# Moving VectorE's side work behind a step's products, and one modulation into the second cycle

## The chip, the cores and the metric

One core of one Trainium2 chip runs the program. The metric is the device time of one execution in microseconds (us). A kernel is timed by the median of its executions; for the kernel before there are three, with a median of 704.68 us (703.97 to 706.22).

## The reference: what is computed

A block with adaptive layer normalization: a state-space convolution over 2048 tokens of 448 channels, then a token-mixing MLP. Six vectors that scale and shift (`sa, ca, ga, sb, cb, gb`, here `mod[0]` to `mod[5]`) come from one condition vector.

```python
mod = (_silu(c) @ w_mod).reshape(c.shape[0], 6, 1, -1)
sa, ca, ga, sb, cb, gb = (mod[:, 0], ..., mod[:, 5])
h = _layernorm(x, axis=-1) * (1 + ca) + sa
x = x + ga * _A_ref(h, ...)     # y = irfft(rfft(u) * rfft(K)), K = 2 Re sum_n C_n exp(A_n dt t)
h = _layernorm(x, axis=-1) * (1 + cb) + sb
x = x + gb * _B_ref(h, ...)     # (W2 gelu(W1 LayerNorm(h)^T))^T over tokens
```

## The kernel before, in words

The convolution's kernel K has 256 complex exponentials for each of 448 channels and 2048 positions. The program makes it in 56 steps `s`, in seven cycles of eight; a step makes the tables of 16 channels for one half of their exponentials. Spectra are multiplied later. A cycle opens with a window (`window(s)`, s a multiple of 8), in which ScalarE (ACT) makes eight magnitudes `mag` by Exp, so that its function table is changed once; then follow eight steps that use Sin. In step s

- `st_abs(s)` and the first lines of `st_step(s)` (L640, L641, L650 to L653) run on ACT: from the phases `xe` and `xg` in PSUM they make two tables `gs` in SBUF and, in place, sines and cosines in `xe` and `xg`;
- GpSimd (POOL) multiplies `mag` by the two `gs` into `G` (L655, L656), and makes the next-but-one step's squared table `m` (`st_mag2`, L630, L632; also called m2);
- VectorE (DVE) makes the four products E(s): two from the sine `xe` (L657, L658), two from the cosine `xg` (L662, L663);
- TensorE (PE) makes kg from E and G of step s-2 (`st_kgen`, L686, 32 small matmuls) and then the phases of step s+1 (`st_phase`, L603). Phase tiles have two PSUM buffers each, so phase s+1 writes where phase s-1 stood, and has to wait for the last product E(s-1) that reads it.

PE, ACT, DVE and POOL issue in the order in which the program is written (a manual schedule). An instruction that waits therefore holds all that stands behind it on its engine. SyncE's DMA queue (SP) is written by hand up to step 8, and ordered by the scheduler after that.

Beside the products there is other work. `between()` in `main`'s loop flushes pending DVE pieces (`dve`: the skip term `ks` L705, rows `yt` L532), takes the statistics of rows of x (`u_stats`, two instructions L503 and L504 a row; 16 rows, the first four in window 0), and advances by `more(n)` a chain of some 50 small DVE instructions that prepares the next parameters (L393 to L452). In the first cycle `between()` stands between the second and the third product of a step; in the second cycle and from step 32 on it stands behind the fourth (`behind`). The statistics of all rows end in `rs` on ACT (L464, L465) and `nm` on DVE (L508 to L512) at the head of window 8; from there POOL and ACT normalize the rows (`u_norm`, L519, L517), PE transforms them (`u_rows`, L529, `pu`) and DVE multiplies them into `yt`.

`modulation(k, *halves)` makes `mod[k]`: two matmuls a half on PE (L490) against a 784 KB slice `wm` of `w_mod`, into one PSUM tile, and one ACT instruction behind the second half (L494). That tile is one of three buffers (`pms`) that `pu` and the second transform `y1` (L724) share. The slices are loaded by `wm_load` (L326), from POOL's queue in the first cycle, into four slots or, late, into rows of the tile `xt` that held x. A row of x is loaded with others by `x_load` (L301), on POOL's queue too.

Of the kernel before, what the change touches and what calls it, by code (L numbers as in the profile page):

```python
# [30 lines left out]
BATCH = 8  # L31
# [194 lines left out]
def tile_adaln_s4d_mixer(ctx, tc, i, out):  # L226
    nc = tc.nc
# [19 lines left out]
    with ExitStack() as es:  # L247
        V, S, G, T = nc.vector, nc.scalar, nc.gpsimd, nc.tensor
# [40 lines left out]
        PP = 112  # L289
# [6 lines left out]
        xt = xp.tile([P, 16, D], F32, name="xt")  # L296
# [27 lines left out]
        def wm_load(k, tile, eng=nc.sync):  # L324
            wms[k] = tile
            eng.dma_start(wms[k], i["w_mod"][:, k * D : (k + 1) * D].rearrange("(q p) d -> p q d", p=PP))  # L326

        s2_v = i["S2"].rearrange("p (k m) -> p k m", k=32)
        svt = sp2.tile([P, 17], F32, name="svt", bufs=1)
# [4 lines left out]
        for q in range(4):  # L334
            r = slice(32 * q, 32 * q + 1)
            nc.sync.dma_start(dskr[r], i["A_D_skip"].rearrange("(o d) -> o d", o=1))

        def wm_slot(k):
            w = wm0.rearrange("p k d -> p (k d)")[0:PP]
            return w[:, 4 * D * (k % 4) : 4 * D * (k % 4 + 1)].rearrange("p (q d) -> p q d", q=4)  # L340
# [2 lines left out]

        late = {
            2: lambda: wm_load(2, wm_slot(2), G),
            3: lambda: wm_load(3, wm_slot(3), G),
            5: lambda: wm_load(0, wm_slot(0), G),
            6: lambda: [
                nc.sync.dma_start(wu, i["WU"]),
                nc.sync.dma_start(wc, i["WC"].rearrange("p (c m) -> p c m", c=2)),  # L350
            ],
            9: lambda: nc.sync.dma_start(svt, i["SV"]),
            10: lambda: [s2_load(0), s2_load(1)],
            11: lambda: [s2_load(2), s2_load(3)],
            12: lambda: wm_load(4, xt[0:PP, 0:4]),
            13: lambda: wm_load(5, xt[0:PP, 4:8]),
        }


# [125 lines left out]
        def modulation(k, *halves):  # L485
            if 0 in halves:
                pmods[k] = pms.tile([P, D], F32, tag="ms", name="pm")
            for h in halves:
                for q in (2 * h, 2 * h + 1):
                    T.matmul(pmods[k], scb[:, q], wms[k][:, q], start=q == 0, stop=q == 3)  # L490
            if 1 not in halves:
                return
            pm = pmods.pop(k)
            act.append(lambda: S.activation(mod[k], pm, AF.Copy, bias=1.0 if k in (1, 4) else 0.0))  # L494
# [6 lines left out]
        def u_stats(r):  # L501
            st = xp.tile([P, 6], F32, tag="st", name="st", bufs=2)
            V.bn_stats(st, xt[:, r])  # L503
            V.bn_aggr(mv[:, r], st)  # L504
# [36 lines left out]
        def s2_load(n):  # L541
            s2s[n] = sp2.tile([P, 2, P], F32, tag="s2", name="s2", bufs=4)
            nc.sync.dma_start(s2s[n], s2_v[:, 2 * n : 2 * n + 2])
# [100 lines left out]
        def st_step(s, between):  # L644
            me, mg_, m2 = v32(mags[s][:, 0]), v32(mags[s][:, 1]), m2s.pop(s)
            E = gp_.tile([P, 2, GD, NJ], F32, tag="E", name="E")
            Gt = gp_.tile([P, 2, GD, NI], F32, tag="G", name="G")

            xe, xg, ab, sg, cg_ = args.pop(s)
            S.activation(xe, xe, AF.Sin, scale=TWO_PI)  # L650
            S.activation(sg, xg, AF.Sin, scale=-TWO_PI)  # L651
            S.activation(cg_, cg_, AF.Sin, scale=-TWO_PI, bias=math.pi / 2)  # L652
            S.activation(xg, ab, AF.Sin, scale=-TWO_PI, bias=math.pi / 2)  # L653
            se, ce = v32(xe), v32(xg)
            G.tensor_tensor(Gt[:, 1], mg_, v32(sg), ALU.mult)  # L655
            G.tensor_tensor(Gt[:, 0], mg_, v32(cg_), ALU.mult)  # L656
            V.tensor_tensor(E[:, 1, :, 32:64], m2, se, ALU.mult)  # L657
            V.scalar_tensor_tensor(E[:, 1, :, 31::-1], me[:, :, 31::-1], -1.0, se, ALU.mult, ALU.mult)  # L658
            behind = s // BATCH == 1 or s >= 32
            if not behind:  # L660
                between()
            V.tensor_tensor(E[:, 0, :, 31::-1], me[:, :, 31::-1], ce, ALU.mult)  # L662
            V.tensor_tensor(E[:, 0, :, 32:64], m2, ce, ALU.mult)  # L663
            if behind:
                between()
            eg[s] = (E, Gt)
            mags.pop(s)
# [371 lines left out]

        WPACE = [[0] * 8, [0, 2, 3, 4, 5, 5, 5, 5], [0, 5, 4, 4, 4, 4, 4, 4], [2] * 8]  # L1040
        pace = [2] * 32
        tail = NHALF + 3
        for s in range(tail):
            if s == 32:
                early.close()
                fp = es.enter_context(tc.tile_pool(name="fp", bufs=2, reuse_waits="tile"))
                m2p.append(right("m2l", BATCH - 3))
                yks[1] = fp.tile([P, 32, DC], F32, name="yk1", bufs=1)
                for n in range(3):
                    pc_load(n)  # L1050
                t0 = fp.tile([P, 2, P], F32, name="t0", bufs=1)
                nc.sync.dma_start(t0, i["T0"].rearrange("p (j m) -> p j m", j=2))
            if s % 2 == 0 and 0 < s and s // 2 + 2 < NG:
                load(s // 2 + 2, False)
            if s == 8:
                first.close()
            if s in late:
                late[s]()
            if s < NHALF and s % BATCH == 0:
                window(s)  # L1060
                if s == 0:
                    gp_ = right("gp", 3)
            if s % BATCH == 4:
                for g in range(s // 2 + 2, min(s // 2 + 6, NG)):
                    load(g, True)

            def between():
                flush(dve)
                if s == 9:
                    tt(mod[0], mod[0], mod[2], ALU.mult)  # L1070
                if 2 <= s < BATCH:
                    for r in range(2 * s, 2 * s + 2):
                        u_stats(r)
                if s < len(pace):
                    more(pace[s])

            mellow()
            if s // BATCH == 1 or s >= NHALF:
                flush(dve)
            if s >= NHALF:  # L1080
                flush(late_act)
                flush(dve)
                mellow()
            else:
                st_abs(s)
                flush(late_act)
                if s < 32 and s % BATCH > 1:
                    st_kgen(s - 2)
                if s % BATCH == 0:
                    if s == 16:  # L1090
                        for k in (4, 5):
                            modulation(k, 0, 1)
                    elif s == 24:
                        some(u_cols, cols, 3)
                    elif s >= 32:
                        piece(False)
                if (s + 1) % BATCH:
                    st_phase(s + 1)
                elif s + 1 < NHALF:
                    st_exponents(s + 1)  # L1100

                if s > 32 and s % BATCH:
                    st_kgen(s - 1)
                st_step(s, between)
            flush(act)
            if s == NHALF:
                st_kgen(s - 1)


            if s < 2:  # L1110
                x_load(4 + 4 * s, 4 + 4 * s, G)
            free = s > 7 and not st_s1(s % BATCH == BATCH - 1)
            if s + 2 < 32 and (s + 2) % BATCH > 1:
                st_mag2(s + 2)

            if 1 < s < 8:
                modulation(s // 2, s % 2)
            if s == 7:
                par_load(2)

            if 8 <= s < 16 and free:
                some(u_rows, rows, 1)
            if s == 12:
                par_load(3)
            if s == 16:
                spec.close()
                up = early.enter_context(tc.tile_pool(name="up", bufs=3, reuse_waits="tile"))
                for n in range(4):
                    u_load(n)
            if 17 <= s < 32 and free:  # L1130
                some(u_cols, cols, 2 if s < 24 else 3)
            if s == 31:
                flush(dve)
                flush(act)
            if s > 32:
                go = pieces[0] < NP and (s % 2 == 1 or s >= NHALF)
                piece(go, None, go or s >= NHALF)
            if s == 34:

                for t in (ft, b1, b2):  # L1140
                    V.memset(t, 0.0)
                nc.sync.dma_start(ft, i["FT"])
                nc.sync.dma_start(b1, i["B_b1"].rearrange("(t p) -> p t", p=P))
                nc.sync.dma_start(b2, i["B_b2"].rearrange("(t p) -> p t", p=P))
# [163 lines left out]
    with ExitStack() as es:  # L1308
        es.enter_context(tc.manual_schedule(engines={ENG.PE, ENG.Activation, ENG.DVE, ENG.Pool}))
        V, S, G = nc.vector, nc.scalar, nc.gpsimd  # L1310
# [73 lines left out]
        for t in range(16):  # L1384
            ss = slice(t * P, (t + 1) * P)
            xt = ru.tile([P, D], F32, tag="x2", name="x2")
# [42 lines left out]
```

## Time and profile before

| | |
|---|---|
| median of three executions | 704.68 us |
| profiled execution | 708.53 us, its span 706.3 us |
| busy: PE / DVE / ACT / POOL | 620.9 / 453.7 / 438.6 / 271.5 us |
| first cycle's steps 0 to 7 | about 28 to 74 us |
| window 8 and second cycle's steps 8 to 15 | about 74 to 131 us |
| MLP, on PE alone | from about 415 us |

The rows of a timeline have a start, a duration, the engine, the source line, the operation and its tiles, and in brackets the idle time of the engine just before with what ended it ("issue" is where the profile shows nothing that ended it). Times are microseconds from the start of the span. A table by stretches gives each engine's busy time in a stretch, the TensorE clock that was granted as a share of full speed, and the busy share of the DMA engines.

### The profile page before, as it was taken

What the parts mean: (1) busy time and instruction counts of PE and PEld (TensorE: products, weight loads), DVE (VectorE), ACT (ScalarE), POOL (GpSimd) and SP (SyncE); (2) the same over time, 40 slices, a digit from 0 to 9 for tenths busy, and PEclk for the clock granted to TensorE, in tenths of its full rate; (3) what the DMA queues carried; (4) which work ended last, traced back from release to release, by engine and by line L of the source; (5) the groups of instructions that cost most, each with busy time, mean ns of one, the idle gap of its engine ahead of it and who ended that gap; (6) DMA issues with size and microseconds to landing.
All of it is one profiled execution on the core that took longest, in us unless ns stands there. A gap on an engine that the chain in (4) does not pass through costs nothing. (4 is left out here: it accounts for less than half of the span.)

```text
span 706.3 us, 18230 instructions
## 1 busy us (share of the span) xinstructions
PE 620.9 (88%) x7164; PEld 461.2 (65%) x7164; DVE 453.7 (64%) x877; ACT 438.6 (62%) x876; POOL 271.5 (38%) x326
## 2 busy tenths in 40 slices
PE   0659878889988779798989779999999999999997
PEld 0335445545534556565566647778999999999996
DVE  7469799889679468595866368777622263344441
ACT  5937698888877699998964458888422242222220
POOL 6486548449358768988776300000000000000000
PEclk9968999999998789999899989999999999999999
DMA  7695464468795425444247989984674445555540
GB/s 172 205 192 136 159 216 163 163 219 257 228 301 174 153 73 140 142 131 140 82 118 220 277 226 250 245 202 125 188 226 141 143 128 159 157 156 157 170 131 27
DMA packets 104051, 121.69 MB, mean 172 GB/s; under 512 B 12730, under 2 KB 91758, under 8 KB 103838
## 3 DMA queue, kind: packets, MB, share of 16 engines
q1 hardware_dynamic: 102430, 113.66, 56.1%
q0 software_dynamic: 1536, 6.87, 4.4%
q8 instruction: 57, 0.93, 0.6%
q14 instruction: 28, 0.23, 0.1%
HBM read 85.14 MB, written 34.87 MB: 170 GB/s over the span
## 5 line engine op out<-in xcount | busy, mean ns | idle before, releaser
L211 ACT CAST whi<-w 128x896 fp32r<-128x896 f32 x64 | 59.8, 939 | 135.5 <-PE o L1396 84.7
L655 POOL TENSOR_TENSOR G<-mag,gs 128x512 f32<-128x512 f32 x56 | 72.0, 1286 | 77.7 <-ACT gs L651 77.6
L220 DVE TENSOR_TENSOR wlo<-w,whi 128x896 fp32r<-128x896 f32 x64 | 68.1, 1087 | 40.3 <-ACT whi L211 31.0
L603 PE MATMUL xg<-tab,lph 64*128 64x512 f32 x112 | 66.3, 594 | 21.1 <-issue 7.9
L1326 PE MATMUL acc<-h3h,whi 128*128 128x448 f32 x224 | 83.7, 374 | 0.7 <-ACT h3h L1241 0.7
L1327 PE MATMUL acc<-h3l,whi 128*128 128x448 f32 x224 | 82.3, 368 | 0.0
L686 PEld LDWEIGHTS kg<-E,G 128*32 128x32 f32 x3584 | 59.0, 118 | 35.6 <-issue 16.3
L1328 PE MATMUL acc<-h3h,wlo 128*128 128x448 f32 x224 | 81.5, 364 | 0.0
L1396 PE MATMUL o<-ul,whi 128*128 128x448 f32 x224 | 81.3, 363 | 0.0
L1395 PE MATMUL o<-uh,whi 128*128 128x448 f32 x224 | 81.2, 362 | 0.0
L1397 PE MATMUL o<-uh,wlo 128*128 128x448 f32 x224 | 80.7, 360 | 0.0
L686 PE MATMUL kg<-E,G 128*32 128x64 f32 x3584 | 69.4, 233 | 6.1 <-issue 4.9
L603 PE MATMUL xe<-tab,lph 64*128 64x512 f32 x112 | 65.5, 588 | 10.1 <-ACT gs L652 7.5
L656 POOL TENSOR_TENSOR G<-mag,gs 128x512 f32<-128x512 f32 x56 | 71.9, 1283 | 0.0
L1399 DVE SCALAR_TENSOR_TENSOR y<-o,b,mod 128x448 f32<-128x448 f32 x16 | 10.9, 684 | 80.3 <-PE o L1397 80.3
L632 POOL TENSOR_TENSOR m<-mag,w 128x512 f32<-128x512 f32 x56 | 59.7, 1067 | 6.0 <-DVE E L663 1.5
L657 DVE TENSOR_TENSOR E<-m,xe 128x512 f32<-128x512 f32 x56 | 38.1, 680 | 30.0 <-ACT xe L650 24.0
L640 ACT ACTIVATE ab<-xe 128x512 f32<-128x512 f32 x56 | 34.0, 606 | 31.7 <-PE xe L603 16.6
L1326 PEld LDWEIGHTS acc<-h3h,whi 128*128 128x128 f32 x224 | 42.6, 190 | 14.3 <-issue 3.3
L603 PE MATMUL xe<-tab,lex 64*128 64x512 f32 x56 | 32.8, 598 | 19.4 <-DMA lex<-wm 17.3
L614 ACT ACTIVATE mag<-xe 128x512 f32<-128x512 f32 x56 | 35.5, 633 | 17.0 <-PE xe L603 6.6
L1328 PEld LDWEIGHTS acc<-h3h,wlo 128*128 128x128 f32 x224 | 42.5, 190 | 3.0
(235 smaller groups left out, 1471.6 us busy)
## 6 DMA issues: line engine op xcount, KB each, us to landing
w<-in_B_w_dram SPq DMA_DIRECT2D x64, 224.0 KB
w<-in_B_w_dram SPq DMA_DIRECT2D x32, 448.0 KB
yu_d<-yt SPq DMA_DIRECT2D x16, 448.0 KB
yi<-yu_d SPq DMA_DIRECT2D x16, 448.0 KB
us_d<-uo SPq DMA_DIRECT2D x16, 448.0 KB
u<-us_d SPq DMA_DIRECT2D x32, 224.0 KB
v_d<-vt SPq DMA_DIRECT2D x32, 224.0 KB
vt<-v_d SPq DMA_DIRECT2D x14, 448.0 KB
```

The costliest lines, as they stand in the source:

```text
L211: self.nc.scalar.copy(hi, w)
L220: eng.tensor_tensor(lo, w, hi.bitcast(F32), ALU.subtract)
L603: T.matmul(out[k], lhs[r], rhs[r], start=start, stop=stop)
L655: G.tensor_tensor(Gt[:, 1], mg_, v32(sg), ALU.mult)
L656: G.tensor_tensor(Gt[:, 0], mg_, v32(cg_), ALU.mult)
L686: T.matmul(kgs[g][32 * q : 32 * q + 32, m], Gt[:, c, d], E[:, c, d], start=h == 0 and c == 0 and m == 0, stop=h == 1 and c == 1, skip_grou ...
L1326: nc.tensor.matmul(acc[f], hi[:, fs], h3h[:, r], start=r == 0, stop=False)
L1327: nc.tensor.matmul(acc[f], hi[:, fs], h3l[:, r], start=False, stop=False)
L1328: nc.tensor.matmul(acc[f], lo[:, fs], h3h[:, r], start=False, stop=r == 15)
L1395: nc.tensor.matmul(o, hi[:, ks], uh[kh][:, k], start=kh == 0 and k == 0, stop=False)
L1396: nc.tensor.matmul(o, hi[:, ks], ul[kh][:, k], start=False, stop=False)
L1397: nc.tensor.matmul(o, lo[:, ks], uh[kh][:, k], start=False, stop=kh == 1 and k == 6)
```

## The change

Three things are moved; no instruction is added or taken away but for how they are split over rows.

1. `between()` stands behind the fourth product in the first cycle too.
2. Statistics come a step later: rows 4 and 5 in step 3 instead of 2, and so on, rows 12 to 15 in step 7.
3. `mod[3]` is made in steps 12 and 13 instead of 6 and 7, from a slice that SP loads into rows 0 to 3 of `xt` from step 9 on; `mod[2]` is made in one piece behind step 6 instead of in steps 4 and 5. The slice of `mod[0]` takes the place of that of `mod[3]` in POOL's queue (step 3), so that step 5 has no load; the slices of `mod[4]` and `mod[5]` go to rows 4 to 7 and, when `mod[3]` has been made, to rows 0 to 3.

```diff
         late = {
             2: lambda: wm_load(2, wm_slot(2), G),
-            3: lambda: wm_load(3, wm_slot(3), G),
-            5: lambda: wm_load(0, wm_slot(0), G),
+            3: lambda: wm_load(0, wm_slot(0), G),
...
-            9: lambda: nc.sync.dma_start(svt, i["SV"]),
+            9: lambda: [nc.sync.dma_start(svt, i["SV"]), wm_load(3, xt[0:PP, 0:4])],
...
-            12: lambda: wm_load(4, xt[0:PP, 0:4]),
-            13: lambda: wm_load(5, xt[0:PP, 4:8]),
+            12: lambda: wm_load(4, xt[0:PP, 4:8]),
+            14: lambda: wm_load(5, xt[0:PP, 0:4]),
...
-            behind = s // BATCH == 1 or s >= 32
+            behind = s < 16 or s >= 32
...
+        mod_steps = {2: (1, 0), 3: (1, 1), 6: (2, 0, 1), 12: (3, 0), 13: (3, 1)}
+        late_rows = {3: (4, 5), 4: (6, 7), 5: (8, 9), 6: (10, 11), 7: (12, 13, 14, 15)}
...
-                if 2 <= s < BATCH:
-                    for r in range(2 * s, 2 * s + 2):
-                        u_stats(r)
+                for r in late_rows.get(s, ()):
+                    u_stats(r)
...
-            if 1 < s < 8:
-                modulation(s // 2, s % 2)
+            if s in mod_steps:
+                modulation(*mod_steps[s])
```

Two places show how rows move. The first is DVE in steps 2 and 3 of the first cycle; E_507 is the product tile of step 2, E_583 (in the change E_577) that of step 3, xe_424 and xg_425 the phases of step 2, st the statistics, ya, t and s the parameter chain. Before:

```order
L657 TENSOR_TENSOR E_507<-m2_417,xe_424 128x16x32
L658 SCALAR_TENSOR_TENSOR E_507<-mag_297,xe_424 128x16x32
L503 BN_STATS st_517<-xt_133 128x6
L504 BN_AGGR mv_175<-st_517 128x2
L503 BN_STATS st_520<-xt_133 128x6
L504 BN_AGGR mv_175<-st_520 128x2
L401 TENSOR_TENSOR ya_399<-ya_399,xa_398 128x256
L404 TENSOR_SCALAR t_401<-s_400 128x256
L662 TENSOR_TENSOR E_507<-mag_297,xg_425 128x16x32
L663 TENSOR_TENSOR E_507<-m2_417,xg_425 128x16x32
L657 TENSOR_TENSOR E_583<-m2_454,xe_497 128x16x32
L658 SCALAR_TENSOR_TENSOR E_583<-mag_304,xe_497 128x16x32
```

The same place in the change (its lines from 355 on are one less):

```order
L656 TENSOR_TENSOR E_507<-m2_417,xe_424 128x16x32
L657 SCALAR_TENSOR_TENSOR E_507<-mag_297,xe_424 128x16x32
L661 TENSOR_TENSOR E_507<-mag_297,xg_425 128x16x32
L662 TENSOR_TENSOR E_507<-m2_417,xg_425 128x16x32
L400 TENSOR_TENSOR ya_401<-ya_401,xa_400 128x256
L403 TENSOR_SCALAR t_403<-s_402 128x256
L656 TENSOR_TENSOR E_577<-m2_454,xe_497 128x16x32
L657 SCALAR_TENSOR_TENSOR E_577<-mag_304,xe_497 128x16x32
L661 TENSOR_TENSOR E_577<-mag_304,xg_498 128x16x32
L662 TENSOR_TENSOR E_577<-m2_454,xg_498 128x16x32
L502 BN_STATS st_589<-xt_133 128x6
L503 BN_AGGR mv_175<-st_589 128x2
```

The four statistics instructions and two of the chain no longer stand ahead of the last two products of step 2; the statistics stand behind all products of step 3.

The second place is PE in step 12: the end of the phases of step 13 (xe_1537, xg_1538; in the change 1531, 1532), the row transform pu, kg, and the first of the next phases. Before:

```order
L603 MATMUL xe_1537<-tab_123,lph0_142 128x512
L603 MATMUL xg_1538<-tab_123,lph0_142 128x512
L529 MATMUL pu_1566<-xt_133,wu_159 128x448
L529 MATMUL pu_1567<-xt_133,wu_159 128x448
L686 MATMUL kg_1504<-E_1461,G_1462 32x64 x32
L603 MATMUL xe_1619<-tab_123,lph1_143 128x512
```

In the change:

```order
L602 MATMUL xe_1531<-tab_123,lph0_142 128x512
L602 MATMUL xg_1532<-tab_123,lph0_142 128x512
L489 MATMUL pm_1559<-xt_133,scb_174 128x448 x2
L528 MATMUL pu_1563<-xt_133,wu_159 128x448
L528 MATMUL pu_1564<-xt_133,wu_159 128x448
L685 MATMUL kg_1498<-E_1455,G_1456 32x64 x32
L602 MATMUL xe_1615<-tab_123,lph1_143 128x512
```

Half a modulation now stands ahead of the row transform of step 12, and in the same way another half in step 13.

## The prediction

> **What bounds the kernel now.** I call the products of step s E(s), its phases phase(s). I read the waits of each engine in the first cycle first. PE's longest there:
>
> ```profile
> PE xg L603 <- issue: 7.9, 1, 7.9
> ```
>
> One wait of 7.9 us, for which the profile names no releaser. The table by stretches around it:
>
> ```profile
> 36.00:43.50 7.50, 7.50 (x145) 4.51 (x142) 4.31 (x6) 4.67 (x9) 7.39 (x11) 0.79 0.91 191
> 43.50:51.50 8.00, 0.12 (x3) 0.05 (x3) 5.59 (x9) 1.91 (x4) 6.44 (x8) 0.66 0.97 195
> 51.50:58.00 6.50, 6.50 (x59) 3.31 (x63) 6.43 (x13) 3.63 (x7) 3.66 (x4) 0.50 0.87 174
> ```
>
> The columns are PE, weight loads, DVE, ACT, POOL, then granted clock, DMA share and GB/s. PE stands still for 8 us, ACT for most of them (1.91 busy), and PE runs at half clock for the 6.5 us behind it. PE's timeline and DVE's, side by side:
>
> ```profile
> 43.10 0.50 PE L603 MATMUL xe<-tab,lph 64*128 64x512 f32 x1
> 51.48 0.76 PE L603 MATMUL xg<-tab,lph 64*128 64x512 f32 x1 [7.88 <-issue]
> ```
>
> ```profile
> 39.66 0.68 DVE L658 SCALAR_TENSOR_TENSOR E<-mag,xe 128x512 f32<-128x512 f32 x1
> 45.84 0.63 DVE L503 BATCH_NORM_STATS2 st<-xt 128x6 f32<-128x448 f32 x1 [5.50 <-DMA xt<-in_A_u_dram]
> ...
> 47.34 2.60 DVE L401 TENSOR_TENSOR ya<-ya,xa 128x256 f32<-128x256 f32 x1
> ...
> 50.10 0.68 DVE L662 TENSOR_TENSOR E<-mag,xg 128x512 f32<-128x512 f32 x1
> 50.70 0.67 DVE L663 TENSOR_TENSOR E<-m,xg 128x512 f32<-128x512 f32 x1
> ...
> 62.03 0.69 DVE L657 TENSOR_TENSOR E<-m,xe 128x512 f32<-128x512 f32 x1 [1.47 <-issue]
> ...
> 72.83 0.18 DVE L504 BATCH_NORM_AGGREGATE mv<-st 128x2 f32<-128x6 f32 x1
> ...
> 74.56 0.18 DVE L508 TENSOR_TENSOR nm<-rs 128x16 f32<-128x16 f32 x1 [0.38 <-ACT rs L465]
> ```
>
> phase(4) on PE wrote `xe` and stopped at `xg`, whose buffer the last two products of E(2) read. DVE had the first two done at 40.34; then came the statistics of rows 4 and 5, whose load landed at 45.84, and the chain. E(2) ended at 51.37, and PE went on at 51.48. So a DMA, through DVE's order, holds PE for 7.9 us. From there to the window DVE hardly rests:
>
> ```profile
> 40.30:74.50 34.20, 25.25 (x381) 13.32 (x380) 26.50 (x52) 20.47 (x43) 23.82 (x26) 0.80 0.71 163
> ```
>
> 26.50 busy of 34.20: of the 7.7 us of idle, 5.50 + 1.47 + 0.38 = 7.35 are the three bracketed rows. DVE bounds the first cycle, and L508 at 74.56 opens the window's row work. The second cycle, by stretches:
>
> ```profile
> 114.00:118.00 4.00, 4.00 (x56) 2.74 (x44) 4.00 (x9) 1.86 (x4) 3.08 (x4) 0.57 0.31 115
> 118.00:122.00 4.00, 4.00 (x119) 2.82 (x120) 4.00 (x8) 3.97 (x9) 2.61 (x3) 1.00 0.47 158
> 122.00:126.00 4.00, 3.95 (x117) 2.74 (x105) 4.00 (x8) 4.00 (x9) 3.65 (x4) 1.00 0.39 146
> 126.00:131.00 5.00, 3.18 (x88) 2.02 (x92) 5.00 (x11) 4.98 (x12) 2.52 (x2) 1.00 0.50 176
> ```
>
> DVE is full in all four, but PE is too, from 114 to 126, and has 5.00 - 3.18 = 1.82 us to spare only behind 126.
>
> **The products first (first part of the change).** The products of E(2) no longer stand behind the statistics. E(2)'s last two take 1.2 (0.60 from start to start in the rows above) and end near 41.5, so phase(4) goes on right behind its first half at 43.6, and the wait on PE goes. What is late next? I follow DVE. The cosine of step 3 is made on ACT here:
>
> ```profile
> 44.98 0.59 ACT L653 ACTIVATE xg<-ab 128x512 f32<-128x512 f32 x1
> ```
>
> That hangs on POOL, not on PE (ACT's sine ahead of it waited for POOL's G), so it stays, and E(3) ends at 45.6 + 1.2 = 46.8; then rows 4 and 5 (landed by 45.84) to 48.4, E(4) with ks and rows 6 and 7 to 53.3, E(5) to 55.7. Then rows 8 and 9 stand in line, with their DMA:
>
> ```profile
> 38.53 2.00 POOL L301 DMA_DIRECT2D xt<-in_A_u_dram  x4
> ```
>
> ```profile
> DMA to landing us min/median/max: 4.3/9.3/17.2
> ```
>
> The second row is the tile xt. Four loads bring rows 8 to 15; the last is issued 1.5 behind 38.53, at 40.03. I take the longest landing, 17.2, since this is the stretch of the DMA engines' highest share (0.97): 57.2. The change keeps these loads where they are. So about 1.5 us of the old wait stays, at another row. From 57.2 DVE has only work, priced by the groups of that stretch:
>
> ```profile
> L503 DVE BATCH_NORM_STATS2 st<-xt 128x6 f32<-128x448 f32 x12 | 7.3, 606 | 5.5 <-DMA xt<-in_A_u_dram 5.5
> L504 DVE BATCH_NORM_AGGREGATE mv<-st 128x2 f32<-128x6 f32 x12 | 2.2, 182 | 0.4
> L705 DVE TENSOR_TENSOR ks<-ks,dsk 128x4 f32<-128x4 f32 x2 | 1.9, 928 | 0.0
> ```
>
> A row of statistics is 0.606 + 0.182 = 0.79. Rows 8 and 9 1.58, E(6) 4 x 0.60 = 2.40, ks 0.93, rows 10 and 11 1.58, E(7) 2.40, rows 12 to 15 3.16: 12.05, so 69.25. The statistics are now the last thing of the cycle, where before E(7)'s last products were, so ACT's two small `rs` instructions come behind them:
>
> ```profile
> 71.31 0.44 ACT L473 ACTIVATE xa<-ya 128x256 f32<-128x256 f32 x1
> ...
> 73.98 0.29 ACT L464 ACTIVATE rs<-mv,eps_t 128x16 f32<-128x16 f32 x1
> 74.31 0.22 ACT L465 ACTIVATE rs<-rs 128x16 f32<-128x16 f32 x1
> ```
>
> 0.55 with the hand-over: L508 at 69.8 instead of 74.56. First term: **4.8 us earlier**. Its ends: 7.35, when rows 8 and 9 land in time and no other wait comes; 2.6 by the first rival. Where the chain's instructions stand costs nothing of its own: they were on DVE and stay there, once per step.
>
> **Modulations out of the first cycle.** Two fewer halves on PE, no POOL issue in step 5 (0.76 in the row at 41.87 below): PE and POOL end before DVE, so I price these at nothing; DVE's 12 us of unbroken work covers them. A copy of mod[3] leaves window 8 for step 14 of ACT, under the same cover.
>
> **Modulation 3 in steps 12 and 13.** Each half is priced by the first of these rows of PE; the second is the same work at half clock:
>
> ```profile
> 60.20 1.77 PE L490 MATMUL pm<-wm,scb 112*128 112x448 f32 x4
> ```
>
> ```profile
> 53.48 3.35 PE L490 MATMUL pm<-wm,scb 112*128 112x448 f32 x4
> ```
>
> PE gets 2 x 1.77 = 3.54 us more where it has no gap until 126, and 1.82 of gap up to 131. What is queued behind: pu of steps 12 and 13, kg, the next phases. Who waits: DVE, for pu,
>
> ```profile
> 119.43 1.14 DVE L532 TENSOR_TENSOR yt<-pu,mod 128x448 f32<-128x448 f32 x2
> ...
> 133.97 1.16 DVE L532 TENSOR_TENSOR yt<-pu,mod 128x448 f32<-128x448 f32 x2 [2.53 <-PE pu L529]
> ```
>
> whose rows at 119.43 now find pu late, and at 133.97 wait for PE already: whatever PE is late by at 131 moves that row. Second term: 3.54 - 1.82 = **1.7 us later**. Its ends: 0, if DVE's other work covers it; 3.5, if PE's gap isn't usable. The held PSUM tile leaves two buffers for pu for two steps; pu then waits for the yt of the step before, which DVE does first in a step (119.43 against a pu in the next step after 120), so nothing more. SP gets loads of 784 KB behind steps 9 and 13; the latter waits for PE's second half, at some 124, and behind it stand a `yu_d` store that needs DVE at about that time and loads for steps 18 on: nothing. The last slice must land by step 16, 20 us later, and took
>
> ```profile
> DMA to landing us min/median/max: 8.2/16.0/17.8
> ```
>
> (the tile wm): in time.
>
> [...] The stretch 114 to 118 has a clock of 0.57 although PE's longest idle just before is short:
>
> ```profile
> 112.53 1.02 PE L529 MATMUL pu<-xt,wu 64*128 64x448 f32 x2 [1.28 <-DVE yt L532]
> ```
>
> [...]
>
> **The sum.** 4.8 - 1.7 = 3.1 us off a span of 706.3: 703.2, the profiled execution 705.4 instead of 708.53. That one lies 3.85 above the median of the runs; from 704.68 the same 3.1 gives **701.6 us**. Behind 131 the engines wait for each other, not for anything fixed in time, and the MLP is PE's alone, so I take it that the shift reaches the end.
>
> **The rivals.**
>
> *A, the one-piece modulation 2 holds the window.* It stands on PE ahead of kg(5), priced at half and at full clock by
>
> ```profile
> 56.76 1.94 PE L686 MATMUL kg<-E,G 128*32 128x64 f32 x64
> ...
> 61.90 1.10 PE L686 MATMUL kg<-E,G 128*32 128x64 f32 x64
> ```
>
> On ACT its copy stands ahead of ks, arctan, the table load and `rs`. Its slice is issued at
>
> ```profile
> 41.87 0.76 POOL L326 DMA_DIRECT2D wm<-in_w_mod_dram  x1
> ```
>
> and lands 16.0 to 17.8 later, at 57.9 to 59.7, when PE has had phase(7) for some 2 us. At full clock 3.54 and kg 1.1 end by 64.4, ks and the 2.67 from arctan to `rs` (71.31 to 73.98) by 67.5: hidden under DVE's 69.25. At half clock 6.70 and kg 1.94 end at 68.3, `rs` at 71.4, L508 at 72.0: 2.6 us earlier instead of 4.8. Net 0.9: 703.8. For it: clocks between 0.50 and 0.79 up to 58 us. Against: PE's long idle is gone. [...] Chance 0.16.
>
> *B, slower: a half-clock stretch lies over modulation 3.* If the 0.57 of 114 to 118 lasts until kg of step 14, the halves cost 2 x 3.35 = 6.70, and PE's work between these rows doubles:
>
> ```profile
> 118.35 1.10 PE L686 MATMUL kg<-E,G 128*32 128x64 f32 x64
> ...
> 122.46 0.50 PE L603 MATMUL xe<-tab,lph 64*128 64x512 f32 x1
> ```
>
> 6.70 + 4.1 - 1.82 = 9.0 later, net 4.2 slower: 708.9. It decides where it passes 4.8. For: the row 0.57. Against: the stretch ended at 118 with PE busy, and the change makes PE busier. Chance 0.06.
>
> *C, PE did not wait for E(2).* The releaser is unnamed; if it was the load of the phases' rows, the first term is gone and 1.7 stays: 706.4. For: "issue". Against: 51.37 and 51.48 fit to 0.11, and that load was issued long before:
>
> ```profile
> 28.85 0.53 SPq L593 DMA_DIRECT2D lph<-pars  x1
> ```
>
> Chance 0.06.
>
> *D, both terms at their better ends.* Rows 8 and 9 land early and DVE covers modulation 3: 7.35 less: 697.3. Against: the landing times. Chance 0.08.
>
> **How the numbers follow.** My forecast has 0.64; halfway from each value to its ends, the first term is 3.7 to 6.1 and the second 0.9 to 2.6, so its own range is a gain of 1.1 to 5.2, 699.5 to 703.6. 0.3%, 2.1 us, is about what can be told from no change here. Four fifths of the forecast lie beyond it, with D: faster 0.60. A, and a fifth of the forecast: same 0.28. B and C: slower 0.12. The range leaves out most of D below and B and C above: 698.4 to 704.9.
>
> **What would show it.** Right: no PE idle over 3 us between 28 and 57; a DVE wait of 1 to 2 us at the statistics of row 8 near 56; L508 near 69.8, released by ACT's `rs` with DVE's statistics just before it; the DVE row of yt in step 12 with up to 1 us of idle from PE; the row now at 133.97 some 3 us earlier. Wrong: a PE stall of the old size at phase(4) (C), the copy of mod[2] on ACT waiting for PE beyond 65 (A), a step 12 or 13 of over 6 us on PE (B), or a shift of the window that is gone at the MLP's first matmul.

## The result, and the profile after

The change makes the kernel faster: 698.94 us in the median of 20 executions against 704.08 of 20 of the kernel before, a ratio of 0.9944 (95% interval 0.9921 to 0.9966), so 3.9 us less (2.4 to 5.6). The ratio leaves disturbed executions out, so it is nearer to 1 than the two medians are. The prediction said 701.6, at 3.1 us less. The profiled execution took 698.92 us, its span 696.9; that of the kernel before took 708.53. The difference of these two, 9.6 us, is more than the change is worth, and the first experiment shows why.

In the rows of the change lines from 355 on are one less than before. The table by stretches of the change, where TensorE had stood still for 8 us (columns as in the prediction: span, PE, weight loads, DVE, ACT, POOL, granted clock, DMA share, GB/s):

```profile
36.00:43.50 7.50, 6.47 (x117) 3.56 (x110) 6.46 (x11) 3.90 (x8) 7.39 (x11) 1.00 0.88 183
43.50:51.50 8.00, 4.94 (x140) 2.94 (x140) 5.58 (x11) 6.00 (x13) 7.83 (x9) 1.00 1.03 204
51.50:58.00 6.50, 4.71 (x69) 2.92 (x71) 5.25 (x13) 5.65 (x12) 6.42 (x8) 0.51 0.93 173
58.00:66.00 8.00, 7.80 (x31) 3.37 (x21) 7.86 (x18) 3.34 (x7) 6.04 (x6) 0.55 0.18 57
```

The stall is gone: PE works 4.94 us of the second row instead of 0.12. The longest wait of PE between 28 and 57 us is the first of its waits (sum, times, longest):

```profile
PE xe L602 <- ACT xg L652: 1.7, 1, 1.7
PE kg L685 <- POOL G L655: 1.5, 1, 1.5
```

But the clock is at half from 51.5 to 66. VectorE in the same execution:

```profile
57.90 0.63 DVE L502 BATCH_NORM_STATS2 st<-xt 128x6 f32<-128x448 f32 x1 [1.18 <-DMA xt<-in_A_u_dram]
...
68.60 0.18 DVE L503 BATCH_NORM_AGGREGATE mv<-st 128x2 f32<-128x6 f32 x1
70.79 0.18 DVE L507 TENSOR_TENSOR nm<-rs 128x16 f32<-128x16 f32 x1 [2.01 <-ACT rs L464]
```

Row 8 waits 1.18 us for its load, and the statistics end at 68.78 where 69.25 was forecast. Yet `nm` comes only at 70.79, after 2.01 us of waiting for ScalarE. What held ScalarE, on PE and on ACT:

```profile
60.67 5.53 PE L489 MATMUL pm<-wm,scb 112*128 112x448 f32 x8 [0.20 <-DMA wm<-in_w_mod_dram]
72.98 1.86 PE L528 MATMUL pu<-xt,wu 64*128 64x448 f32 x3 [4.06 <-POOL xt L518]
```

```profile
66.23 0.54 ACT L493 ACTIVATE mod<-pm 128x448 f32<-128x448 f32 x1 [2.57 <-PE pm L489]
67.30 0.37 ACT L699 COPY ks<-kg 128x256 f32<-128x256 f32 x1 [0.52 <-PE kg L685]
...
70.22 0.29 ACT L463 ACTIVATE rs<-mv,eps_t 128x16 f32<-128x16 f32 x1
70.54 0.22 ACT L464 ACTIVATE rs<-rs 128x16 f32<-128x16 f32 x1
```

Modulation 2's slice has landed by 60.67, its four matmuls (eight rows of the trace) take 5.53 us at a clock of 0.50 up to 65.24 and 1.00 behind it, its copy waits for them, and behind the copy stand `ks`, the table load (1.28 us at 67.99) and `rs`. This is the prediction's rival A, in part. In the second cycle the rows of `yt` from step 11 on:

```profile
112.82 1.14 DVE L531 TENSOR_TENSOR yt<-pu,mod 128x448 f32<-128x448 f32 x2
116.27 1.15 DVE L531 TENSOR_TENSOR yt<-pu,mod 128x448 f32<-128x448 f32 x2
120.86 1.14 DVE L531 TENSOR_TENSOR yt<-pu,mod 128x448 f32<-128x448 f32 x2
124.31 1.15 DVE L531 TENSOR_TENSOR yt<-pu,mod 128x448 f32<-128x448 f32 x2
130.47 1.16 DVE L531 TENSOR_TENSOR yt<-pu,mod 128x448 f32<-128x448 f32 x2 [1.36 <-PE pu L528]
```

None of those beside modulation 3 waits for PE, and the one that stood at 133.97 with 2.53 us of wait is at 130.47 with 1.36.

### The profile page after: what moved, and what is told of

Same layout as the page of the kernel before. It is cut to its first block, busy times and chain, and to the rows that moved or that the text cites. A ratio compares the mean times of both kernels' runs of the same rounds, so it can differ in the third digit from the quotient of the medians.

```text
span 696.9 us, 18228 instructions
## 1 busy us (share of the span) xinstructions
PE 620.1 (89%) x7164; PEld 459.4 (66%) x7164; DVE 453.9 (65%) x877; ACT 438.0 (63%) x876; POOL 270.4 (39%) x325
## 5 line engine op out<-in xcount | busy, mean ns | idle before, releaser
L602 PE MATMUL xe<-tab,lph 64*128 64x512 f32 x112 | 67.0, 601 | 9.6 <-ACT gs L651 6.9
L1397 PEld LDWEIGHTS o<-uh,wlo 128*128 128x128 f32 x224 | 42.0, 188 | 3.2
```

The costliest lines, as they stand in the source:

```text
L602: T.matmul(out[k], lhs[r], rhs[r], start=start, stop=stop)
L1397: nc.tensor.matmul(o, lo[:, ks], uh[kh][:, k], start=False, stop=kh == 1 and k == 6)
```

## The experiments

Twelve kernels were run, each against the kernel before on the same chip. To read their traces alike I take distances between starts of rows: from the first product of step 0, E(0), to `nm` (the end of what the first term speaks of), to E(8) (window 8 added), from E(10) to E(16) (which holds modulation 3's steps), and from the first product of x, `pu`, in window 8 to E(8). All in us.

| kernel | ratio to before | 95% interval | E(0) to nm | E(0) to E(8) | pu to E(8) | E(10) to E(16) |
|---|---|---|---|---|---|---|
| before | | | 44.81 | 67.16 | 20.16 | 41.27 |
| the change | 0.9944 | 0.9921 to 0.9966 | 40.71 | 64.25 | 21.35 | 42.16 |
| control | 0.9988 | 0.9952 to 1.0025 | 43.84 | 65.15 | 19.12 | 41.42 |
| products_first | 1.0062 | 1.0030 to 1.0094 | 49.17 | 71.49 | 20.12 | 41.30 |
| products_and_stats | 1.0084 | 1.0051 to 1.0117 | 49.81 | 72.55 | 20.56 | 42.09 |
| modulations_alone | 0.9999 | 0.9968 to 1.0030 | 45.28 | 69.01 | 21.55 | 40.82 |
| early_slice | 0.9982 | 0.9948 to 1.0016 | 41.44 | 65.10 | 21.39 | 40.32 |
| mod2_later | 0.9925 | 0.9894 to 0.9956 | 40.69 | 63.52 | 20.94 | 42.15 |
| mod3_first_cycle | 0.9938 | 0.9912 to 0.9963 | 39.79 | 63.35 | 18.58 | 42.47 |
| mod3_twice | 0.9946 | 0.9917 to 0.9974 | 39.92 | 62.96 | 20.85 | 42.92 |
| kept_busy | 0.9947 | 0.9923 to 0.9971 | 40.27 | 63.34 | 18.57 | 40.81 |
| rows_later | 0.9924 | 0.9893 to 0.9955 | 39.26 | 61.82 | 20.24 | 42.19 |
| both | 0.9925 | 0.9898 to 0.9953 | 39.72 | 63.82 | 18.57 | 45.21 |
| both_shorter | 0.9958 | 0.9927 to 0.9988 | 39.25 | 60.60 | 19.47 | 41.70 |

My theory after the first comparison of traces was: the products' order brings the gain, the late slice takes some of it back, and the modulations' move is worth nothing or costs a little. The rival: the modulations' move is what gains.

### control: the kernel before, once more

The edit is an empty line.

> The kernel before, once more, for a second trace and a time beside the others. If the rest of the two traces' difference behind the first cycle (7.7 us at E(32), 9.2 us at the MLP's first matmul) is how executions differ, this trace has E(32) some 2 to 5 us earlier than 251.37 while nm (74.56), E(8) (96.91) and E(16) (148.36) stay within 0.5 us; if the change itself makes it, E(32) is within 1 us of 251.37 here too. Time within 0.3% of 704.

Its profiled execution took 699.21 us. The row of E(32), first in the trace of before, then in that of the control:

```profile
251.37 0.69 DVE L657 TENSOR_TENSOR E<-m,xe 128x512 f32<-128x512 f32 x1 [3.66 <-ACT xe L650]
```

```profile
243.24 0.69 DVE L657 TENSOR_TENSOR E<-m,xe 128x512 f32<-128x512 f32 x1 [2.11 <-ACT xe L650]
```

The same code is 8.1 us earlier here in one execution than in the other; the change has this row at 243.69. So the stretch behind E(24), where the two compared traces part by 5.8 us, has nothing to do with the change. That `nm` and E(8) would stay within 0.5 us was wrong: from E(0) they come 1.0 and 2.0 us earlier. Single traces are good to about 1 us at `nm` and 2 us at E(8), no better.

### products_first, products_and_stats, modulations_alone: the parts by themselves

The first has only

```diff
-            behind = s // BATCH == 1 or s >= 32
+            behind = s < 16 or s >= 32
```

> Only the order on VectorE: a step's products ahead of its other work in the first cycle; statistics and modulations where they were. Theory (the step's products were held by statistics that wait for the load of x): the 8 us of idle TensorE at step 2 go, but rows 8 and 9, now behind the products of step 4, wait for the second load of x that lands at 57, so that VectorE loses some 3 us there; nm at 72 to 73 instead of 74.56, and the time 1.5 to 2.5 us below the kernel before. Rival (the gain is the modulations' that left the first cycle): nm within 0.7 of 74.56 and no gain.

the second this line and `late_rows` with its loop,

> VectorE's order and the later statistics, all three modulations still in the first cycle. Theory: nothing on VectorE waits for x for more than 1.5 us, the statistics end near 69, and nm comes at 69.5 to 71.5, since modulation 2's second half is then at steps 5 and 6 and its copy on ScalarE isn't late; no half clock cost and no cost in the second cycle, so 3.5 to 5 us below the kernel before, as good as the change or better. Rival (TensorE has no room for six modulation halves in the faster first cycle): 3.5 us of matmuls of modulation 3 come onto the path, nm at 73 or later, and the gain is under 2 us.

and the third only `mod_steps` with the loads that go with it.

> The modulations moved as in the change, VectorE's order and the statistics as before. Theory: the stall at step 2 stays, VectorE sets nm, which is within 1 us of 74.56; the second cycle carries modulation 3 for at most 1.7 us; time from 0.5 us below to 2 us above the kernel before. Rival (the moved modulations are what gains): nm at 72 or earlier, and 3 us or more below the kernel before.

The third went as expected: the modulations' move alone is worth nothing, 0.9999. But the first two became slower, by 0.62% and 0.84%, which neither theory had. In products_and_stats, on PE and on DVE:

```profile
61.43 3.35 PE L490 MATMUL pm<-wm,scb 112*128 112x448 f32 x4 [13.16 <-DMA wm<-in_w_mod_dram]
```

```profile
57.50 0.63 DVE L503 BATCH_NORM_STATS2 st<-xt 128x6 f32<-128x448 f32 x1 [1.13 <-DMA xt<-in_A_u_dram]
...
69.04 0.69 DVE L657 TENSOR_TENSOR E<-m,xe 128x512 f32<-128x512 f32 x1 [9.97 <-PE pm L490]
```

With E(2) out of the way PE reaches modulation 2 at 48.3, where the kernel before has it at 60.20 without a wait. Its slice lands at 61.4 all the same, and PE stands 13.16 us; phases and kg stand behind it, and DVE waits 9.97 us for them. The 8 us stall of the kernel before had covered this wait. In products_first it is the same slice, at 61.04: PE stands 7.53 us there, and DVE waits 5.0 us for x and 6.1 us behind modulation 2, so `nm` comes at 78.46 where 72 to 73 was expected. So each edit alone gives nothing or a loss, and the two together gain: the products' order needs modulation 2 to stand where its slice has landed. Both theories fall, and the next runs ask whether it is the slice. What the later statistics are worth beside these two was not run.

### early_slice and mod3_first_cycle: is it the slice?

In products_and_stats, with the slice loaded one step sooner:

```diff
-            2: lambda: wm_load(2, wm_slot(2), G),
+            1: lambda: wm_load(2, wm_slot(2), G),
...
-... 5: (8, 9), 6: (10, 11), 7: (12, 13, 14, 15)}
+... 6: (8, 9, 10, 11), 7: (12, 13, 14, 15)}
```

> VectorE's order and the later statistics, with all modulations where the kernel before has them, but modulation 2's slice is loaded one step sooner, ahead of x's last four pieces, and rows 8 and 9 are summed up behind step 6. Theory (products_and_stats lost because TensorE stood 13.2 us at modulation 2, whose slice lands at 61): TensorE's idle there goes below 3 us, from E(0) to nm 41 to 43 us instead of 49.8, and the time is 4 to 9 us below products_and_stats, at or below the kernel before. Rival (it was the six halves on TensorE): nm stays beyond 46 us behind E(0).

```profile
51.64 3.35 PE L490 MATMUL pm<-wm,scb 112*128 112x448 f32 x4 [1.38 <-DMA wm<-in_w_mod_dram]
```

The wait is 1.38 us instead of 13.16, `nm` comes 41.44 us behind E(0) instead of 49.81, and the ratio falls from 1.0084 to 0.9982 (0.9948 to 1.0016). So it was the landing of the slice, not the six halves on PE: they are all still there. With the change's other moves undone it reaches the kernel before, and perhaps a little less; the change is better by 0.4%, with intervals that overlap.

The other way round, the change with modulation 3 back in the first cycle:

```diff
-        mod_steps = {2: (1, 0), 3: (1, 1), 6: (2, 0, 1), 12: (3, 0), 13: (3, 1)}
+        mod_steps = {2: (1, 0), 3: (1, 1), 6: (2, 0, 1), 7: (3, 0, 1)}
```

> The change, with modulation 3 left in the first cycle, behind step 7, and its slice loaded as in the kernel before. Theory (what the order needs is modulation 2 behind step 6 alone): modulation 3's 3.5 us of matmuls fill part of the 4.06 us in which TensorE waits for window 8's first rows, from E(0) to E(8) 63.5 to 65.5 us (64.25 in the change), from E(10) to E(16) 41 to 42.2, time within 0.4% of the change. Rival (both moves count): E(8) 2 us or more later than in the change, and the time 2 to 4 us above it.

0.9938 against 0.9944: no difference. Of the two modulations that move, only modulation 2's place matters. The two distances come out just beyond what was expected, 63.35 from E(0) to E(8) and 42.47 from E(10) to E(16). Modulation 3's rows start at 68.54 and take 4.94 us there, PE has no idle ahead of `pu`, and from `pu` to E(8) it takes 18.58 us instead of 21.35: work that is needed anyway fills the gap ahead of window 8, which the last runs below fill with matmuls that nobody reads.

### mod3_twice: the price of modulation 3 in the second cycle

```diff
-                for q in (2 * h, 2 * h + 1):
-                    T.matmul(pmods[k], scb[:, q], wms[k][:, q], start=q == 0, stop=q == 3)
+                qs = (2 * h, 2 * h + 1) if k != 3 else (0, 1, 0, 1) if h == 0 else (0, 1, 2, 3)
+                for q in qs:
+                    T.matmul(pmods[k], scb[:, q], wms[k][:, q], start=q == 0, stop=q == 3 or k == 3 and h == 0 and q == 1)
```

> The change, with modulation 3's matmuls in steps 12 and 13 issued twice (the result of the first four isn't read), 3.54 us more on TensorE. The prediction's second term (they lie on the path but for a gap of 1.82 us): from E(10) to E(16) 45 to 46 us instead of 42.16, time 3 to 4 us above the change. Rival (TensorE has room there, since the same stretch takes 41.3 to 42.1 us without modulation 3): E(10) to E(16) below 43.2 us and the time within 0.3% of the change.

E(10) to E(16) takes 42.92 us, 0.76 more than in the change, for 3.54 us more of matmuls, and the ratio is that of the change. Where the doubled work shows:

```profile
120.77 1.15 DVE L532 TENSOR_TENSOR yt<-pu,mod 128x448 f32<-128x448 f32 x2 [2.68 <-PE pu L529]
```

DVE waits 2.68 us for the late `pu` of step 13. From E(10) to E(15) it takes 22.69 us, where the change takes 20.86: 1.83 us more. That only 0.76 are left at E(16) does not show that the rest is given back, since behind E(15) the change had 6.8 us at half clock and mod3_twice had none. So PE has room for some half of the added matmuls, not for all of them. For the single modulation the table says: the six traces without it in steps 12 and 13 have 40.32 to 42.47 us from E(10) to E(16) (mean 41.48), the seven with it once 40.81 to 45.21 (mean 42.15, without `both` 41.64). Its price, 0.2 to 0.7 us, is less than the spread of either group.

### mod2_later: rival A taken away

```diff
-        mod_steps = {2: (1, 0), 3: (1, 1), 6: (2, 0, 1), 12: (3, 0), 13: (3, 1)}
+        mod_steps = {2: (1, 0), 3: (1, 1), 6: (2, 0), 7: (2, 1), 12: (3, 0), 13: (3, 1)}
...
-                if s == 8 and e == 0:
+                if s == 8 and e == 1:
                     tt(mod[1], mod[1], mod[2], ALU.mult)
```

> The change, with modulation 2's two halves behind steps 6 and 7 and the product that reads it one element later in window 8, so that ScalarE copies mod[2] behind its two operations for rs. Theory (rival A of the prediction, the late slice holds rs): from E(0) to nm 39.2 to 39.8 us instead of 40.71, limited by the end of the statistics (38.70 us behind E(0)), at a gain of about 1 us that the times of the runs can hardly tell. Rival (something else holds rs, such as kg's products): nm stays at 40.4 to 41.

```profile
57.98 0.63 DVE L502 BATCH_NORM_STATS2 st<-xt 128x6 f32<-128x448 f32 x1 [1.90 <-DMA xt<-in_A_u_dram]
...
69.34 0.18 DVE L503 BATCH_NORM_AGGREGATE mv<-st 128x2 f32<-128x6 f32 x1
70.14 0.18 DVE L507 TENSOR_TENSOR nm<-rs 128x16 f32<-128x16 f32 x1 [0.62 <-ACT rs L464]
```

`rs` is 0.62 us behind the statistics instead of 2.01, so the copy of mod[2] was what held it. But row 8's load came later in this execution (1.90 us of wait), and `nm` stays at 40.69. Rival A's mechanism is shown, its size is not: with the copy out of the way, the load of x is the next thing late.

### rows_later, kept_busy, both, both_shorter: what is still lost

rows_later is mod2_later with rows 8 and 9 one step later, the second edit of early_slice.

> mod2_later with the statistics of rows 8 and 9 one step later, so that VectorE doesn't wait for x's second half. Theory (those 1.90 us of waiting are the last loss ahead of nm): from E(0) to nm 38.6 to 39.4 us instead of 40.69. Rival (VectorE then waits for TensorE, whose modulation 2 waits for its slice until 60): the wait goes to E(6) or E(7), and nm stays at 40 to 41.

The wait for x is gone and `nm` comes 39.26 us behind E(0), as expected. kept_busy puts matmuls that nobody reads into PE's gap ahead of window 8:

```diff
+                if s == 8 and e == 0:
+                    ex = pms.tile([P, D], F32, tag="ms", name="ex")
+                    for n in range(8):
+                        T.matmul(ex, scb[:, n % 4], wms[2][:, n % 4], start=n == 0, stop=n == 7)
```

> mod2_later with eight matmuls more (modulation 2's operands into a tile that nobody reads) on TensorE ahead of window 8's first product of x, to fill the 3.80 us in which it waits for x's first rows. Theory (the idle before window 8 brings a half clock behind it, which cost 1.2 us of VectorE's waits): window 8's products at 1.02 us for four instead of 1.85, granted clock 1.00 from 72 to 78 instead of 0.53 to 0.61, from nm to E(8) 21.3 to 22 us instead of 22.83, time 0.5 to 1.5 us below mod2_later. Rival (the clock falls for another reason than idle time here): clock below 0.7 somewhere between 68 and 78, the eight matmuls take over 5 us and nm to E(8) is 23 us or more.

> kept_busy and rows_later together. Theory: the sum of the two, from E(0) to E(8) 60 to 61.3 us instead of 63.52, time 2 to 3 us below mod2_later, which would be the best of all kernels here. Rival: one of the two only moves its wait, from E(0) to E(8) 62 us or more.

The change from 72 to 78 us, and kept_busy from 68 to 78:

```profile
72.00:75.00 3.00, 2.02 (x6) 0.98 (x6) 0.54 (x3) 1.10 (x3) 3.00 (x5) 0.51 0.10 28
75.00:78.00 3.00, 3.00 (x68) 2.20 (x68) 2.32 (x4) 1.46 (x3) 2.92 (x6) 0.50 0.25 91
```

```profile
68.00:72.00 4.00, 4.00 (x20) 2.10 (x12) 2.46 (x11) 2.80 (x8) 1.12 (x2) 1.00 0.54 159
72.00:75.00 3.00, 3.00 (x13) 1.36 (x11) 0.22 (x1) 0.51 (x2) 2.92 (x5) 1.00 0.09 23
75.00:78.00 3.00, 3.00 (x75) 1.73 (x72) 2.58 (x5) 1.68 (x4) 2.92 (x5) 1.00 0.11 35
```

The clock stays at 1.00, and from the first `pu` to E(8) it takes 18.57 us, where the stretches that begin at half clock have 20.12 to 21.55. But the eight matmuls were too many:

```profile
68.05 6.28 PE L1016 MATMUL ex<-wm,scb 112*128 112x448 f32 x16
74.26 1.02 PE L528 MATMUL pu<-xt,wu 64*128 64x448 f32 x4
```

6.28 us, with the first `pu` at 74.26 instead of 72.03: what the clock gave, the delay took, and `nm` to E(8) took 23.07 us, the rival's number though not by its reason. I had priced one of them at half its cost; each is two rows of the trace. So the sum in `both` failed too: 63.82 us from E(0) to E(8). In the runs neither is faster than mod2_later, as both were expected to be (0.9947 and 0.9925, for 0.9925). Three of them, on rows_later:

> rows_later with three such matmuls instead of kept_busy's eight (one took 0.79 us there, 6.28 for the eight, which was too long for the gap and moved window 8's first product from 72.03 to 74.26). Theory (from the first product of x to E(8) it is 18.6 us at full clock, 20.2 to 21.4 where the stretch begins at half clock): three take 2.6 us and end as the first product is due, so that this stretch is 18.5 to 19.2 us instead of 20.24 in rows_later, and E(0) to E(8) 60.3 to 61.2 us instead of 61.82; time 0.5 to 1.5 us below rows_later, within its interval. Rival (the clock is not set by this gap): the stretch stays at 20 us or more.

```profile
67.92 2.52 PE L1016 MATMUL ex<-wm,scb 112*128 112x448 f32 x6
71.66 1.02 PE L528 MATMUL pu<-xt,wu 64*128 64x448 f32 x3 [1.22 <-POOL xt L518]
```

19.47 us from `pu` to E(8), a little over what I expected, and 60.60 from E(0) to E(8), as expected: 3.65 less than the change. In the time of the runs it doesn't show: 0.9958 (0.9927 to 0.9988). The trace says where it was lost in that execution: from E(0) to the MLP's first product it takes 375.42 us, the change 375.90, the control 376.49. The stretches behind E(16) differ between executions of one kernel by more than these 3.65 us: from E(24) to E(32) before took 52.33 and the control 47.71. Whether a better first cycle is given back later by some rule, or only hidden by this spread, stays open.

rows_later (696.69 us in the median, 0.9924) and mod2_later (698.16, 0.9925) are below the change, but their intervals overlap with its own; a version that beats the change for certain wasn't found.

## Why the prediction was right, and where it was not

**The first term: right in kind, too large.** The products of E(2) did wait for x, and PE for them; rival C is out. A wait of 1 to 2 us stayed at row 8 (1.18), and the statistics ended at 68.78 for 69.25. That is nearer than its parts, and so in part luck: row 8's statistics started 0.7 us later than the 57.2 I had worked out, and DVE's work behind it took 10.88 us instead of 12.05. I had priced `ks` at 0.93, the mean of rows that took 1.25 and 0.61, and it takes 0.16 here. L508 (L507 now) came 3.77 us earlier instead of 4.8; counted from E(0) 4.1, against the control 3.1. What failed is the step "0.55 with the hand-over": ACT's `rs` came 2.01 us behind the statistics, because rival A, given 0.16, came half true. The slice took 18.4 us, longer than the 16.0 to 17.8 that I had from the trace,

```profile
DMA to landing us min/median/max: 16.4/17.4/18.4
```

and the clock was at half. PE's longest wait from 36 to 66 us was 1.5 us, and the clock was 0.51 to 0.55 from 51.5 to 66 all the same: that PE's long idle is gone, the argument against A, did not keep the clock full.

**Modulations out of the first cycle: priced at nothing, and that is the step that failed.** I wrote that PE and POOL end before DVE, and that DVE's 12 us of unbroken work covers them. Alone the move is worth nothing (0.9999). But DVE's work is unbroken only because modulation 2 has left step 4: with it there DVE waits 9.97 us. I costed each edit against the trace of before, where the stall that another edit removes covered the wait for the slice. The first term was worked out with modulation 2 already gone, and that is why this did not spoil the total; its 4.8 us were not the order's alone, as the text had them, but that of the pair.

**The second term: too large.** 1.7 us were forecast for modulation 3 in steps 12 and 13, at full clock, where its halves did run in the change (1.77 us each at 112.14 and 117.53, the clock 1.00 from 110 to 122); the traces show 0.2 to 0.7 (the means of the groups above), and doubling it adds 1.83 up to E(15) instead of 3.5. The step that failed is that PE has no room before 126. In the trace of before PE was busy at 4.00 of 4.00 from 114 to 118 at a clock of 0.57, and it stayed full at full clock up to 126, with what that stretch had left. The same code in the control, with its slow stretch ahead of these steps, leaves PE 2.4 us:

```profile
110.00:114.00 4.00, 2.92 (x16) 1.27 (x12) 4.00 (x7) 4.00 (x8) 3.90 (x5) 1.00 0.74 243
114.00:118.00 4.00, 3.50 (x81) 2.22 (x84) 4.00 (x8) 2.94 (x7) 3.87 (x5) 1.00 0.45 143
118.00:122.00 4.00, 3.89 (x77) 2.18 (x76) 4.00 (x7) 4.00 (x9) 3.42 (x3) 1.00 0.32 121
122.00:126.00 4.00, 3.31 (x131) 2.41 (x130) 4.00 (x8) 4.00 (x9) 2.40 (x2) 1.00 0.40 129
```

The change's execution had its slow stretch ahead of them too:

```profile
98.00:102.00 4.00, 4.00 (x33) 1.65 (x33) 3.83 (x7) 4.00 (x9) 3.92 (x5) 0.50 0.33 96
102.00:106.00 4.00, 4.00 (x62) 2.51 (x52) 4.00 (x6) 2.89 (x6) 3.92 (x5) 0.50 0.05 15
...
114.00:118.00 4.00, 4.00 (x77) 2.29 (x78) 4.00 (x8) 3.03 (x8) 3.92 (x6) 1.00 0.44 146
```

Here PE's 4.00 of 4.00 us at half clock, or right behind it, did not mean that it was full.

**Rival B** was seen once, in `both`: 0.56 of the clock over the first half of modulation 3 (the second half, from 120.5, ran at full clock), and DVE waits for `pu` in steps 12 and 13,

```profile
110.00:116.00 6.00, 6.00 (x76) 3.42 (x76) 5.99 (x12) 3.86 (x8) 3.69 (x5) 0.56 0.43 157
```

```profile
118.46 1.16 DVE L531 TENSOR_TENSOR yt<-pu,mod 128x448 f32<-128x448 f32 x2 [2.47 <-PE pu L528]
123.25 1.15 DVE L531 TENSOR_TENSOR yt<-pu,mod 128x448 f32<-128x448 f32 x2 [1.17 <-PE pu L528]
```

E(10) to E(16) took 45.21, 3.0 us over the change, not the 9.0 of its price.

**Not in the prediction:** PE's gap ahead of window 8 grew to 4.06 us, the clock fell to half behind it, and of the 3.77 us 1.2 were lost again by E(8) (2.58 earlier). kept_busy and both_shorter show the cause by taking it away: the clock is 1.00 from 68 to 78, and from `pu` to E(8) they take 18.57 and 19.47 us instead of 21.35. In rows_later a shorter wait than those 4.06 us, 2.45 us, had the same behind it, 0.58 of the clock from 72 to 75:

```profile
70.71 1.43 PE L528 MATMUL pu<-xt,wu 64*128 64x448 f32 x3 [2.45 <-DMA wu<-in_WU_dram]
```

```profile
72.00:75.00 3.00, 3.00 (x70) 1.99 (x68) 2.78 (x4) 1.33 (x3) 2.92 (x6) 0.58 0.21 74
```

**The shift to the end** is not shown by the traces. From E(0) to E(8) the change takes 2.9 us less than before, but only 0.9 less than the control, and the runs gain 3.9 (2.4 to 5.6). At the MLP's first product it is 9.5 us less than before, but only 0.6 less than the control, so the last sign that I had named, a shift that is gone there, can't be judged by two traces that differ so much. In the runs the losses arrive: products_first and products_and_stats take 4.3 and 5.4 us more than before from E(0) to E(8) (6.3 and 7.4 more than the control), and 4.4 and 5.9 us more in time (0.62% and 0.84% of 703).

**The total** was in part luck. By the traces the 0.9 to 2.9 us at E(8), less the 0.2 to 0.7 of modulation 3, make 0.2 to 2.7; the runs gain 3.9 (2.4 to 5.6). Both terms of the forecast were too large, with opposite signs, and the loss of clock behind `nm` was not in it, so that 3.1 comes nearer to the measured gain than its parts do to theirs.

## What to carry to other kernels

A stall can cover other waits; here one of 7.9 us covered one of 13.16. Before an edit that removes one is costed, go down the queue of the engine that gets free, and ask of each instruction whether its data has landed by the new time; and if a move is priced at nothing, ask whether another term was worked out with it in place. That an engine is busy in a stretch of half clock, or right behind one, is no proof that it has no room there: from 114 to 118 PE was busy for 4.00 us at a clock of 0.57, and for 3.50 at 1.00 with the same code.

## What the hardware did that I had not expected

Half clock came in the change's first cycle, from 51.6 us on, behind waits of PE of at most 1.5 us, and the same two waits ahead of window 8 (1.07 and about 0.93) were followed by half clock in one execution of the kernel before and by full clock in the other:

```profile
76.75 1.86 PE L529 MATMUL pu<-xt,wu 64*128 64x448 f32 x3 [0.93 <-POOL xt L519]
```

```profile
75.11 1.02 PE L529 MATMUL pu<-xt,wu 64*128 64x448 f32 x3 [0.94 <-POOL xt L519]
```

The second is the control. So these short gaps alone didn't decide it. What follows is counted from the traces of this case, from the clock that each records and from PE's rows. In the traces of before and of the change the granted clock is 1.00 or 0.50, and each stretch between two changes is a multiple of 3.41 us: at 0.50 it lasts 3.41, 6.83, 10.24 or 13.65 us. In intervals of this length, over the first 400 us of these two traces, PE was busy for less than half of the time in 17 intervals at full clock, and 16 of them were followed by half clock. Of 14 with 50% to 65% it was 5, and of 147 above that none. In all fourteen traces the same count gives 100 of 108, 34 of 105 and 1 of 1045. In the kernel before both waits fall into one interval, which ends where the half clock begins:

```profile
73.30:76.71 3.41, 1.50 (x65) 1.12 (x65) 2.37 (x9) 3.38 (x11) 1.03 (x2) 1.00 0.14 42
76.71:80.12 3.41, 3.37 (x49) 2.06 (x53) 1.48 (x3) 1.64 (x4) 3.33 (x6) 0.50 0.00 0
```

In the control the grid lies otherwise, and each interval has one of them:

```profile
70.48:73.90 3.42, 2.35 (x63) 1.19 (x65) 2.87 (x11) 3.38 (x9) 0.61 (x1) 1.00 0.50 141
73.90:77.31 3.41, 2.48 (x90) 1.69 (x79) 1.79 (x6) 2.67 (x6) 3.27 (x5) 1.00 0.06 19
```

By the same count the change's half clock from 51.6 us on stands behind an interval with 1.54 of 3.41 us busy, made of several short waits, and the one ahead of window 8 behind 0.27 of 3.42. The 0.57 from 114 us on, ahead of which PE's longest idle is short (1.28 us), stands behind 2.13 of 3.41, in the middle group. So in these traces half clock went with the sum of the waits in an interval (1.91 us of 3.41 in the row of before, 1.07 and 0.93 in those of the control) more than with the longest of them. Why the clock does so was not shown, and no run moved the grid on purpose. With the gap filled the clock stayed at 1.00 from 68 to 78 us in kept_busy, both and both_shorter.
